# Four transformer layers on one core: half of the last output projection accumulated in PSUM ahead of the last group, and one wait for all norms

## The chip, the core and the metric

The kernel runs on one core of a Trainium2 chip. The core has a matrix engine (TensorE; in the profile PE for matmuls and PEld for weight loads), VectorE (DVE), ScalarE (ACT), GpSimd (POOL) and SyncE (SP), which issues transfers. They share SBUF; TensorE writes its results to PSUM, eight banks of 128 x 512 floats, which VectorE and ScalarE read. Each engine runs its own instructions in order and waits on semaphores for the others.

The metric is the device time of one execution in microseconds (us), the median of several runs: 2148.82 us before.

## What is computed

One sequence of 2048 rows with 640 features goes through four layers, A, B, A, B, each with a layer norm, an attention of 32 heads of 20 features, an output projection and a residual. Layer kind A lets a row see the last 256 rows only, kind B all rows. Shortened:

```python
def _B_ref(x, wqkv, wo):          # _A_ref: the same, with a window of 256
    qkv = (x @ wqkv).reshape(B, S, 3, H, Dh)
    q, k, v = ...
    scores = jnp.einsum("bhqd,bhkd->bhqk", q, k) * (Dh ** -0.5)
    p = _softmax(scores, axis=-1)
    o = jnp.einsum("bhqk,bhkd->bhqd", p, v)
    return o.transpose(0, 2, 1, 3).reshape(B, S, D) @ wo

x = x + _A_ref(_layernorm(x, axis=-1), A_wqkv, A_wo)
x = x + _B_ref(_layernorm(x, axis=-1), B_wqkv, B_wo)
x = x + _A_ref(_layernorm(x, axis=-1), A_wqkv, A_wo)
x = x + _B_ref(_layernorm(x, axis=-1), B_wqkv, B_wo)
```

## The kernel before

**Tiling.** Rows are cut into 4 chunks (c) of 512, a chunk into 4 row blocks (qb) of 128. Heads are cut into 8 groups (g) of 4 heads. In SBUF a group's 4 heads of 20 features stand on 4 strips of 32 partitions; small matmuls with 32 columns of weights go to the four strips of a bank side by side (the helper `by_columns`, L317 to L321). A unit of attention is one (layer, chunk, group), or a part of its keys; layers 1 and 3 see all keys, 64 score blocks of 128 keys x 512 queries for a whole unit.

**The main loop** (L1442) goes through the units in a fixed order, written out at L780 to L796, and one pass is a tile: 2 to 4 score blocks. A tile's scores go to PSUM banks 0 to 2 (even tiles) or 3 to 5 (odd tiles; a fourth block in bank 6), ScalarE turns them into exponentials with one instruction (L1515), and two or three tiles later the product with the values is summed in bank 7 (`op`, L1547). At a unit's end `finish_unit` copies bank 7 to SBUF (L924) and pushes a tail. Besides, VectorE computes some of the exponentials itself, by a chain of cheap instructions, two blocks at a time (the "side" blocks: L1031 reads the scores, L1047 to L1069 do the rest). A block is given to it only when a count of VectorE's backlog kept while the program is written (`state["lag"]`) is low and, from layer 3, chunk 1 on, when bank 6 is free.

**Tasks.** All else is a Python generator that yields after a few instructions: tails first, then `todo` in the order of need. `pump` (L271) advances them in each tile as far as a credit allows: `yield ("pe", n)` and `("hold", n)` cost n, after a hold the same task goes on at once, and `("wait", n)` puts the task to sleep for n tiles. So the program is one fixed order of instructions for each engine; a wait of a task is no semaphore, it only sets how far down in the order the next instructions stand. From layer 3, chunk 1 on the credit is 0.45 a tile. A task that needs a PSUM bank takes it from `mfree` with `take_m` (L286): from the end of the early stage that is bank 6 alone, and after the last tiles banks 1 to 5 as well (L1612). `keep_clock` and `warm_bank` put matmuls in whose result is not read, so that TensorE stays busy.

**The norm** (`t_ln`, L434): GpSimd computes 1/sqrt(variance + eps) in two instructions (L441, L444), the task sleeps 4 tiles in layers 0 and 1 and 2 tiles in layers 2 and 3 (L445), then VectorE computes the shift (L447) and the normed rows (L455), TensorE transposes them (L475) and VectorE copies them out. Then follow the value pieces (`t_v`) and the projections to keys and queries (`t_block`), whose results GpSimd writes to DRAM (L532, L575) and SyncE loads as units need them (L820 to L842).

**The tail of a unit** (`t_tail`, L1169): the sums of the softmax stand among the outputs; TensorE gathers them with selector strips (`sel4`), VectorE takes reciprocals (L1191) and splits each into two bf16 numbers (L1195, L1196), TensorE transposes them (L1204), VectorE copies (L1211), TensorE spreads them over the strips (`spread8`), and VectorE multiplies (L1232). In the very last tail `fill` puts dummy matmuls into bank 0 between these steps: 2, 3, 1 and 3. `settle` (L1237) then packs the strips of layer 3's later chunks densely with small transfers, and groups 6 and 7 of the last chunk stay in strips.

**The output projection** (`t_out`, L585) of a chunk sums over all groups for each row block and each half (i) of 320 output columns, adds the residual on VectorE (L607), and in layer 3 SyncE stores the row block (L613). For the last chunk it is cut in two: after group 5 is packed, `t_before_last` (L621) sums groups 0 to 5 in four dense matmuls for each of 8 pieces (L630), adds the residual and puts the float sums in `part_o` (L639); after the last group `t_out` does groups 6 and 7 with 8 strips a piece and adds them.

Of the kernel before, what the change touches and what calls it, by code (L numbers as in the profile page):

```python
# [15 lines left out]
ALU = mybir.AluOpType  # L16
ACT = mybir.ActivationFunctionType

P = 128
S = 2048  # L20
D = 640
# [3 lines left out]
KD = D // P  # L25
G = 8
C = 512
NC = S // C
EPS = 1e-5
SCALE = DH ** -0.5  # L30
HD = D // 2
# [27 lines left out]
def kernel(  # L59
# [10 lines left out]
    nc = tc.nc  # L70
# [22 lines left out]
    xout = out.flatten_outer_dims().rearrange("(t p) d -> p t d", p=P)  # L93
# [27 lines left out]
    op = ps[:, 7, :]  # L121
# [21 lines left out]
    def packed(l, c):  # L143

        return l == 3 and c > 0
# [58 lines left out]
    ready = set()  # L204
# [112 lines left out]
    def by_columns(out_, lhsT, rhs, start, stop):  # L317

        for j in range(lhsT.shape[-1] // 32):
            r = slice(32 * j, 32 * j + 32)  # L320
            nc.tensor.matmul(out_[r], lhsT=lhsT[:, r], rhs=rhs, start=start, stop=stop)  # L321
# [112 lines left out]
    def t_ln(l, c):  # L434
# [7 lines left out]
            out=rstd[:], in0=mv[:, :, 1], scalar1=EPS, scalar2=1.0, op0=ALU.add, op1=ALU.mult  # L442
        )
        nc.gpsimd.tensor_tensor(out=rstd[:], in0=rstd[:], in1=nhalf[:], op=ALU.pow)  # L444
        yield ("wait", 4 if l < 2 else 2)  # L445
        nmr = lnp.tile([P, 4], F32, name="nmr", tag="nmr")
        nc.vector.scalar_tensor_tensor(  # L447
            out=nmr[:], in0=mv[:, :, 0], scalar=-1.0, in1=rstd[:], op0=ALU.mult, op1=ALU.mult
# [136 lines left out]
    def t_out(l, c):  # L585
        on = ons[l, c]
        last = (l, c) == (3, NC - 1)
        while last and "before_last" not in ready:
            yield ("wait", 1)
        assert out_seq[out_n[0]] == l % 2  # L590
        dense = packed(l, c) and not last
        a, b = (0, KD) if dense else (G - 2 if last else 0, G)
        for qb in range(4):
            for i in range(2):
                mb = yield from take_m()
                yp = ps[:, mb, 0:HD]
                for g in range(a, b):
                    by_columns(
                        yp, on[:, g, qb * P : (qb + 1) * P],
                        wop[:, g, i * HD : (i + 1) * HD], g == a, g == b - 1,  # L600
                    )
                    if g < b - 1:
                        yield ("hold", 0.14)
                xv = x_sb[:, 4 * c + qb, i * HD : (i + 1) * HD]
                had = part_o["t"][:, 2 * qb + i, 0:HD] if last else xv
                state["lag"] += 0.5
                nc.vector.tensor_tensor(out=xv, in0=had, in1=yp, op=ALU.add)  # L607
                drop_m(mb)
                yield ("pe", 0.14)
            if l < 3:  # L610
                stats(l + 1, c, qb)
            else:
                nc.sync.dma_start(out=xout[:, 4 * c + qb, :], in_=x_sb[:, 4 * c + qb, :])  # L613
        ons.pop((l, c))
        ready.add(("out", l, c))
        ready.add(("x", l + 1, c))
        n = out_n[0] = out_n[0] + 1
        if n < len(out_seq) and (n == 13 or out_seq[n] != out_seq[n - 1]):
            load_wop(out_seq[n], n >= 13)

    def t_before_last():  # L621

        on = ons[3, NC - 1]
        for qb in range(4):
            for i in range(2):
                mb = yield from take_m()
                yp = ps[:, mb, 0:HD]
                for b in range(4):
                    n = min(P, (G - 2) * 80 - b * P)
                    nc.tensor.matmul(  # L630
                        yp, lhsT=on[0:n, b, qb * P : (qb + 1) * P],
                        rhs=wop[0:n, b, i * HD : (i + 1) * HD],
                        start=(b == 0), stop=(b == 3),
                    )
                    if b < 3:
                        yield ("hold", 0.14)
                xv = x_sb[:, 4 * (NC - 1) + qb, i * HD : (i + 1) * HD]
                state["lag"] += 0.5
                nc.vector.tensor_tensor(  # L639
                    out=part_o["t"][:, 2 * qb + i, 0:HD], in0=xv, in1=yp, op=ALU.add  # L640
                )
                drop_m(mb)
                yield ("pe", 0.14)
        ready.add("before_last")

    def push_layer(l, c):

# [521 lines left out]
    def t_tail(us):  # L1169
        final = us[-1][0:3] == (3, NC - 1, G - 1)  # L1170

        def fill(count):

            for n in range(count * final):
                nc.tensor.matmul(  # L1175
                    ps[:, 0, :], lhsT=ident[:], rhs=masks[:, 0, :], start=True, stop=True
                )

        n = len(us)
        yield ("wait", 2)  # L1180
# [56 lines left out]
    def settle(l, c, g, oT):  # L1237
# [128 lines left out]
    with tc.manual_schedule():  # L1366
# [75 lines left out]
        while ended is None or t < ended + 8:  # L1442
# [204 lines left out]
```

## Time and profile before

| | |
|---|---|
| median of 3 runs | 2148.82 us (2148.77 to 2149.24) |
| profiled execution, its own time | 2151.47 us |
| its span, first to last instruction | 2149.8 us |
| mean granted TensorE clock | 0.998 |
| ScalarE, exponentials (L1515) | 2052.5 us in 1643 instructions |
| side blocks of VectorE (L1031) from 522 us on | 307 |
| last exponential ends | 2138.55 us |
| last add of the projection ends | 2146.80 us |

The page of the profile has the busy time of each engine, the span in 40 slices, the DMA queues, the chain of work that ended last and the costliest groups of instructions. A group's line reads: source line, engine, operation, output and inputs by name, shape, count, then busy us and mean ns of one, then idle time of the engine just before and what ended it. Other answers from the same trace are used too: waits by engine, the timeline of an engine in a stretch (start us, duration us, instruction, and in brackets idle time before it), and busy times by stretch, where after the stretch and its length come PE, PEld, DVE, ACT and POOL with the number of instructions, the granted clock, the busy share of DMA and GB/s.

### The profile page before, as it was taken

The numbers are of one execution on the slowest core, as the hardware profiler recorded it, in microseconds if no ns is written. First come the engines' busy times: TensorE is split into PE (matmuls) and PEld (weight loads), VectorE is DVE, ScalarE is ACT, GpSimd is POOL, SyncE is SP. The second block draws the span as 40 slices with busy tenths as digits, with TensorE's granted clock in tenths as the row PEclk, the third lists the DMA queues.
The fourth block names the chain that finished last, engine by engine and source line by source line (L and its number), as shares of the span: only waits on it lengthen the run. The fifth ranks groups of instructions, "written<-read, shape, count | busy, mean of one in ns | idle before, by whom it ended". The sixth has DMA issues, their size and how long they took to land. (4 is left out here: it accounts for less than half of the span.)

```text
span 2149.8 us, 73242 instructions
## 1 busy us (share of the span) xinstructions
PE 1925.2 (90%) x31735; PEld 755.9 (35%) x31736; DVE 1445.1 (67%) x2699; ACT 2088.4 (97%) x1723; POOL 366.2 (17%) x808
## 2 busy tenths in 40 slices
PE   8999999988899888888988989898898988888898
PEld 4444443433333333333333433343322222222222
DVE  5566664426677676776767643773588888887886
ACT  7899999999999999999999999999999999999998
POOL 6553433100130003300033001510000000000000
PEclk9999999999999999999999999999999999999999
DMA  6422221321210112111220112111121111111100
GB/s 203 124 76 54 75 60 51 77 66 43 62 47 25 54 53 78 29 33 47 57 82 21 38 55 76 33 48 52 54 63 39 33 36 42 33 33 42 44 25 16
DMA packets 84080, 117.07 MB, mean 54 GB/s; under 512 B 21646, under 2 KB 65966, under 8 KB 83758
## 3 DMA queue, kind: packets, MB, share of 16 engines
q1 hardware_dynamic: 73598, 82.05, 14.5%
q0 software_dynamic: 10160, 30.36, 4.0%
q8 instruction: 248, 4.06, 0.8%
q14 instruction: 74, 0.61, 0.1%
HBM read 77.56 MB, written 28.77 MB: 49 GB/s over the span
## 5 line engine op out<-in xcount | busy, mean ns | idle before, releaser
L1515 ACT ACTIVATE pt<-ps 128x1536 bf16<-128x1536 f32 (+3 forms) x1643 | 2052.5, 1413 | 33.6 <-PE ps L1489 24.5
L1489 PE MATMUL ps<-qt,kt 32*128 32x512 bf16 x3913 | 545.7, 384 | 62.3 <-ACT pt L1515 54.9
L321 PE MATMUL ps<-masks,ident 128*32 128x512 bf16 x5720 | 512.3, 384 | 92.8 <-ACT pt L1515 47.8
L1547 PE MATMUL ps<-pt,vt 128*21 128x512 bf16 x3782 | 377.7, 386 | 0.3 <-ACT pt L1515 0.2
L1489 PEld LDWEIGHTS <-kt 32*128 32x128 bf16 x3913 | 155.4, 91 | 460.2 <-issue 441.6
L321 PEld LDWEIGHTS <-ident 128*32 128x32 bf16 x5720 | 182.2, 94 | 282.6 <-issue 256.5
L1587 POOL TENSOR_SCALAR_AFFINE_SELECT pt<-pt 128x256 bf16<-128x256 bf16 (+2 forms) x513 | 221.3, 453 | 199.6 <-ACT pt L1515 183.5
L1547 PEld LDWEIGHTS <-vt 128*21 128x21 bf16 x3782 | 93.7, 89 | 256.4 <-issue 253.0
L354 DVE CAST st<-ps 128x512 bf16<-128x512 f32 x128 | 88.4, 691 | 138.1 <-PE ps L321 138.0
L321 PE MATMUL ps<-wop,on 128*32 128x320 bf16 x3712 | 161.6, 300 | 4.4 <-DVE on L1232 2.2
L1031 DVE TENSOR_SCALAR spare<-ps 128x512 int32<-128x512 f32 x200 | 137.4, 687 | 29.9 <-PE ps L1013 27.1
L321 PEld LDWEIGHTS <-on 128*32 128x32 bf16 x5760 | 122.6, 95 | 62.3 <-issue 28.9
L1598 DVE TENSOR_TENSOR pt<-pt,masks 128x512 bf16<-128x512 bf16 (+3 forms) x275 | 117.7, 445 | 32.2 <-ACT pt L1515 30.9
L1489 PE MATMUL ps<-qa,ka 32*128 32x384 bf16 (+2 forms) x1408 | 119.7, 276 | 19.7 <-ACT pt L1515 16.4
L321 PE MATMUL ps<-xnT,spare 128*32 128x512 bf16 x1870 | 128.6, 381 | 3.5 <-ACT xnT L351 0.8
L1232 DVE TENSOR_TENSOR on<-on,ps 128x512 bf16<-128x512 bf16 x128 | 86.6, 685 | 65.1 <-PE ps L321 61.9
L321 PE MATMUL ps<-wv,xnT 128*32 128x320 bf16 x2560 | 115.9, 301 | 9.5 <-DVE on L1232 3.5
L607 DVE TENSOR_TENSOR x_sb<-x_sb,ps 128x320 bf16<-128x320 bf16 x120 | 58.4, 486 | 98.2 <-PE ps L321 97.0
L1031 DVE TENSOR_SCALAR raw_o<-ps 128x512 int32<-128x512 f32 x114 | 78.3, 687 | 52.5 <-PE ps L1489 51.7
L924 DVE CAST on<-ps 128x512 bf16<-128x512 f32 x112 | 76.9, 687 | 47.0 <-PE ps L1547 41.0
L321 PE MATMUL ps<-xnT,wqk 128*32 128x512 bf16 x1360 | 92.3, 381 | 1.7 <-DVE st L354 0.5
L575 POOL DMA_DIRECT2D k_d<-st x79 | 43.9, 556 | 258.8 <-DVE st L354 234.8
(110 smaller groups left out, 1711.6 us busy)
## 6 DMA issues: line engine op xcount, KB each, us to landing
vt<-v_d SPq DMA_DIRECT2D x48, 336.0 KB
kt<-k_d SPq DMA_DIRECT2D x192, 80.0 KB
k_d<-st POOLq DMA_DIRECT2D x78, 128.0 KB, 2.2
q_d<-st POOLq DMA_DIRECT2D x78, 128.0 KB, 2.1
qt<-q_d SPq DMA_DIRECT2D x384, 20.0 KB
v_d<-vs POOLq DMA_DIRECT2D x16, 336.0 KB, 3.1
qa<-q_d SPq DMA_DIRECT2D x248, 20.0 KB
ka<-k_d SPq DMA_DIRECT2D x248, 20.0 KB
```

The costliest lines, as they stand in the source:

```text
L321: nc.tensor.matmul(out_[r], lhsT=lhsT[:, r], rhs=rhs, start=start, stop=stop)
L354: nc.vector.tensor_copy(out=out_, in_=in_)
L575: nc.gpsimd.dma_start(out=dst, in_=staging.pop()[0 : rows.stop - rows.start])
L607: nc.vector.tensor_tensor(out=xv, in0=had, in1=yp, op=ALU.add)
L924: nc.vector.tensor_copy(out=oT, in_=op)
L1031: nc.vector.tensor_scalar(out=xi.bitcast(I32)[:, i * C : (i + 1) * C], in0=z, scalar1=SCALE * LOG2E * FIX, scalar2=127.5 * FIX, op0=ALU.mu ...
L1232: nc.vector.tensor_tensor(out=oT, in0=oT, in1=zb, op=ALU.mult)
L1489: nc.tensor.matmul(sp[:, i, col * P : (col + qn) * P], lhsT=u.k(kc, j), rhs=u.q(j, q0, qn), start=True, stop=True,)
L1515: nc.scalar.activation(out=pt[:, i:k, b0 * P :], in_=sp[:, i:k, b0 * P :], func=ACT.Exp, scale=SCALE,)
L1547: nc.tensor.matmul(op[32 * j : 32 * j + VW, q0 * P : (q0 + qn) * P], lhsT=u.v(kc, j), rhs=pg[:, i, col * P : (col + qn) * P], start=(first ...
L1587: nc.gpsimd.affine_select(out=v, in_=v, compare_op=ALU.is_gt if later else ALU.is_ge, fill=0.0, base=0, pattern=[[0, k - i], [-1 if later ...
L1598: nc.vector.tensor_tensor(out=pt_[:, i:k, cols], in0=pt_[:, i:k, cols], in1=mv_, op=ALU.mult)
```

## The change

1. **Norms.** The sleep in `t_ln` is 4 tiles in all layers; it was 2 in layers 2 and 3.
2. **Early sums.** `t_before_last` is pushed after group 6 is settled, not after group 5. It does the lower halves only (4 pieces, columns 0 to 319), each with the four dense matmuls of groups 0 to 5 and then four strips of group 6.
3. **Upper halves.** A new generator, `upper_halves`, fills banks 1 to 4, one for each row block: the residual by a matmul with the identity, the four dense matmuls, and the strips of group 6: 24 steps. `fill` in the last tail now takes three of these steps where it put one dummy (6, 9, 3 and the rest).
4. **The end.** A new `t_last` takes the place of `t_out` for the last chunk. For each row block it adds the four strips of group 7 to the upper half in its bank and ScalarE copies that to the output row; four strips of group 7 give the lower half, which VectorE adds to the early sum. Then the row block is stored.
5. After the last tiles `mfree` gets banks 0 and 5, not 1 to 5.

```diff
-        yield ("wait", 4 if l < 2 else 2)
+        yield ("wait", 4)
...
     def t_out(l, c):
         on = ons[l, c]
         last = (l, c) == (3, NC - 1)
-        while last and "before_last" not in ready:
-            yield ("wait", 1)
+        if last:
+            while "before_last" not in ready:
+                yield ("wait", 1)
+            yield from t_last(on)
+            return
...
+    def early_groups(yp, qb, i, start):
+        on = ons[3, NC - 1]
+        q, f = slice(qb * P, (qb + 1) * P), slice(i * HD, (i + 1) * HD)
+        def dense(b):
+            n = min(P, (G - 2) * 80 - b * P)
+            nc.tensor.matmul(
+                yp, lhsT=on[0:n, b, q], rhs=wop[0:n, b, f], start=start and b == 0, stop=False,
+            )
+        def strips():
+            by_columns(yp, on[:, G - 2, q], wop[:, G - 2, f], False, start)
+        return [lambda b=b: dense(b) for b in range(4)] + [strips]
+
     def t_before_last():
-        on = ons[3, NC - 1]
+        while ("tail", 3, NC - 1, G - 3) not in ready:
+            yield ("wait", 1)
         for qb in range(4):
-            for i in range(2):
...
+            mb = yield from take_m()
+            yp = ps[:, mb, 0:HD]
+            for n, step in enumerate(early_groups(yp, qb, 0, True)):
+                step()
+                if n < 4:
+                    yield ("hold", 0.14)
+            state["lag"] += 0.5
+            nc.vector.tensor_tensor(
+                out=part_o["t"][:, qb, 0:HD], in0=x_sb[:, 4 * (NC - 1) + qb, 0:HD], in1=yp,
+                op=ALU.add,
+            )
+            drop_m(mb)
+            yield ("pe", 0.14)
         ready.add("before_last")
+
+    def upper_halves():
+        for qb in range(4):
+            yp = ps[:, 1 + qb, 0:HD]
+            nc.tensor.matmul(
+                yp, lhsT=ident[:], rhs=x_sb[:, 4 * (NC - 1) + qb, HD:D], start=True, stop=False,
+            )
+            yield
+            for step in early_groups(yp, qb, 1, False):
+                step()
+                yield
+    upper = upper_halves()
+
+    def t_last(on):
+        for _ in upper:
+            pass
+        for qb in range(4):
+            row = 4 * (NC - 1) + qb
+            lhsT = on[:, G - 1, qb * P : (qb + 1) * P]
+            yp = ps[:, 1 + qb, 0:HD]
+            by_columns(yp, lhsT, wop[:, G - 1, HD:D], False, True)
+            nc.scalar.copy(out=x_sb[:, row, HD:D], in_=yp)
+            mb = yield from take_m()
+            yp = ps[:, mb, 0:HD]
+            by_columns(yp, lhsT, wop[:, G - 1, 0:HD], True, True)
+            nc.vector.tensor_tensor(
+                out=x_sb[:, row, 0:HD], in0=part_o["t"][:, qb, 0:HD], in1=yp, op=ALU.add
+            )
+            drop_m(mb)
+            nc.sync.dma_start(out=xout[:, row, :], in_=x_sb[:, row, :])
+            yield ("pe", 0.27)
+        ready.add(("out", 3, NC - 1))
...
         def fill(count):
-            for n in range(count * final):
-                nc.tensor.matmul(
-                    ps[:, 0, :], lhsT=ident[:], rhs=masks[:, 0, :], start=True, stop=True
-                )
+            for n in range(3 * count * final):
+                next(upper, None)
...
-        if (l, c, g) == (3, NC - 1, G - 3):
-            push("before_last", t_before_last(), 0, 8.0)
+        if (l, c, g) == (3, NC - 1, G - 2):
+            push("before_last", t_before_last(), 0, 5.0)
...
-        mfree.update((b, (0, 0)) for b in range(1, 6))
+        mfree.update((b, (0, 0)) for b in (0, 5))
```

More of the change, by code (lines that the diff above doesn't have):

```diff
@@ L587, in t_out @@
         last = (l, c) == (3, NC - 1)
-        while last and "before_last" not in ready:
-            yield ("wait", 1)
+        if last:
[3 more added lines that the diff above has]
+            return
         assert out_seq[out_n[0]] == l % 2
-        dense = packed(l, c) and not last
-        a, b = (0, KD) if dense else (G - 2 if last else 0, G)
+        a, b = (0, KD) if packed(l, c) else (0, G)
         for qb in range(4):
@@ L604, in t_out @@
                 xv = x_sb[:, 4 * c + qb, i * HD : (i + 1) * HD]
-                had = part_o["t"][:, 2 * qb + i, 0:HD] if last else xv
                 state["lag"] += 0.5
-                nc.vector.tensor_tensor(out=xv, in0=had, in1=yp, op=ALU.add)
+                nc.vector.tensor_tensor(out=xv, in0=xv, in1=yp, op=ALU.add)
                 drop_m(mb)
```

18 lines of the change are left out of this document (removed).

## The prediction, made before the changed kernel ran

> **What bounds the kernel now.** I began with the page's busy times. ScalarE, which turns score tiles into exponentials (L1515), is the engine nearest to full; its share is over the whole span, so I then asked for its idle time stage by stage and only at the end for the chain of waits of the last 12 us. A line of the first view reads: engine, busy us, share, instructions.
>
> ```profile
> PE 1925.2 (90%) x31735; PEld 755.9 (35%) x31736; DVE 1445.1 (67%) x2699; ACT 2088.4 (97%) x1723; POOL 366.2 (17%) x808
> ```
>
> While scores flow, then, a change is worth only what it adds to or takes from ScalarE's idle time, or the blocks that VectorE takes from it. One block of 512 columns costs ScalarE (1529 - 1081) = 0.45 us, from the mean 1536- and 1024-column exponentials. From 522 us (the first norm that the diff touches) to 1545 us ScalarE is busy 1009.54 of 1023 us, from 1545 to 2119 us 571.10 of 574. So the late norms can win back at most 13.5 us in their own stage, and the projection at the very end works where ScalarE has nothing left to do.
>
> **The late norms.** The view of waits by engine shows three waits of VectorE at L447 for GpSimd's power; listed by time these are 3 of the 8 norms of layers 2 and 3 (two-tile wait), at 698.9, 1209.3 and 1423.2 us. None of the 7 norms of layers 0 and 1 that run in this task (four-tile wait) has one. Around the second, the timelines of VectorE, TensorE and ScalarE, each with the idle time before an instruction and what ended it in brackets:
>
> ```profile
> DVE nmr L447 <- POOL rstd L444: 3.8, 3, 1.4
> ...
> 1209.26 0.16 DVE L447 SCALAR_TENSOR_TENSOR nmr<-mv,rstd 128x4 f32<-128x4 f32 x1 [1.44 <-POOL rstd L444]
> ...
> 1210.08 0.46 PE L475 MATMUL ps<-ident,xn 128*32 128x128 bf16 x20 [0.91 <-DVE xn L455]
> ...
> 1213.22 1.02 ACT L1515 ACTIVATE pt<-ps 128x1024 bf16<-128x1024 f32 x1 [0.80 <-PE ps L1489]
> 1215.70 1.45 ACT L1515 ACTIVATE pt<-ps 128x1536 bf16<-128x1536 f32 x1 [1.45 <-PE ps L1489]
> 1218.17 5.17 ACT L1515 ACTIVATE pt<-ps 128x1536 bf16<-128x1536 f32 x4 [1.02 <-PE ps L1489]
> ```
>
> The reader is to see a relay: GpSimd late, VectorE idle 1.44 us, TensorE idle 0.91 us for the normed row, and two us later ScalarE idle three times, 0.80 + 1.45 + 1.02 = 3.27 us, for scores. Why so much later and so much more? Busy time by stretch, with the granted clock behind the engines:
>
> ```profile
> 1207.00:1211.00 4.00, 2.68 (x49) 1.05 (x46) 2.49 (x8) 4.00 (x5) 1.85 (x4) 1.00 0.70 149
> 1211.00:1217.50 6.50, 6.26 (x95) 2.92 (x90) 2.77 (x6) 3.90 (x4) 0.00 (x0) 0.51 0.09 18
> ```
>
> TensorE was busy only 2.68 of 4.00 us, and then ran 6.5 us at clock 0.51, busy 6.26 of them, while ScalarE was busy 3.90. The halved clock turned a 0.91 us hole into 3.27 us.
>
> The page "TensorE: Matmul & The Clock Gate" of the Trainium skill (Part 1: The HAM clock gate) ties the half clock to at least one idle window of about 3.4 us. Here no idle of that length precedes it: the longest is 0.91 us, so the measurement decides. By the page's rule this hole would not be the cause, and the norms' term below would be 0; that case is the second rival.
>
> *What the four-tile wait does.* No instruction is added. L447, four normed rows (L455), 80 transposes (L475) and four copies are issued two tiles later, 2 x 1.3 = 2.6 us by the pitch of the exponentials (13 in 16.72 us from 690.58). GpSimd's pair (0.19 + 1.04 us) stays where it is and has 2.6 us more. Behind the norm move the value pieces, ten projected blocks, GpSimd's 10 k_d and q_d transfers (and 2 of v_d in layer 3), and SP's loads that read them. Cover: after the norm at 1209 the first k_d transfer leaves at 1232.87 and SP loads the next full unit from 1233.00; the unit before it is closed by VectorE at 1257.44. Twenty us of cover against 2.6. Without it each late us is a us of ScalarE's. Cost taken: 0. Gain taken: the 3.27 us; the other two waits (698.9 and 1423.2) cost ScalarE nothing within 5 us. Bounds: 0 (the hole comes back elsewhere) and 3.27 plus the idle that is left in the two stretches 1205 to 1247 (4.3 in all) and 1421 to 1451 (1.8 + 0.7), which is -6.8.
>
> **The end.** From the chain of waits and the timeline after the last exponential:
>
> ```profile
> 2139.50 0.69 DVE L924 CAST on<-ps 128x512 bf16<-128x512 f32 x1 [1.75 <-PE ps L1547]
> 2140.45 0.82 PE L1175 MATMUL ps<-masks,ident 128*128 128x512 bf16 x3
> 2141.33 0.23 PE L1204 MATMUL ps<-ident,hl 128*32 128x128 bf16 x1
> 2142.95 2.36 PE L321 MATMUL ps<-wop,on 128*32 128x320 bf16 x64
> 2143.53 3.27 DVE L607 TENSOR_TENSOR x_sb<-raw_o,ps 128x320 bf16<-128x320 f32 x8 [0.52 <-PE ps L321]
> 2144.44 2.72 SPq L613 DMA_DIRECT2D out_dram<-x_sb  x4
> ```
>
> TensorE finishes the projection in 2.36 us; eight adds of VectorE take 3.27 and set the end at 2146.80, and the last transfer the rest to 2149.8. ScalarE is idle.
>
> *Removed:* four of the eight adds. Their pitch is (3.27 - 0.48) / 7 = 0.40, so four end 4 x 0.40 = 1.60 us sooner: **-1.60**. *Added on ScalarE:* four copies of 128x320 float to bf16; the early copies of that form (L351, va<-ps) take 0.43 us, so 4 x 0.43 = 1.72 beside four adds of 3 x 0.40 + 0.48 = 1.68, starting four matmuls earlier: hidden, 0; without that lead they cost some 0.05. *Removed on TensorE:* 32 of the 64 strips, not on the path, 0.
>
> *Added on TensorE, ahead of it:* the nine dummies (pitch (0.82 - 0.39) / 2 = 0.215) become 24 real steps. A step is a 320-column matmul, pitch 0.135 from L630 ((0.72 - 0.45) / 2), or four strips at (2.36 - 0.30) / 63 x 4 = 0.13. The path through the final tail then shifts so:
> - Two dummies (0.43) become 6 steps (0.81): +0.38, of which 0.10 was idle before the selector strips at 2140.25: shift 0.28.
> - Three (0.645) become 9 (1.215): +0.57; TensorE was free at 2140.45 + 0.645 = 2141.10 and the transpose began at 2141.33, so 0.23 is absorbed: shift 0.62.
> - One becomes 3: +0.19, of which 0.16 was idle before the spread strips at 2141.86: 0.65.
> - Three become the 6 that are left: +0.165, of which 0.10 idle before 2142.95: 0.72.
>
> So the projection starts at 2143.67, the first add 0.58 later as now, and the last ends at 2143.67 + 0.58 + 1.20 + 0.48 = 2145.93 instead of 2146.80: **-0.87**. Banks 0, 5 and 6 rotate over four lower halves; the fourth waits for the first add, ended by 2144.73, when TensorE needs the bank at about 2144.7: 0. Bounds: -1.60 (no shift) and +0.7 (the full shift, and copies that hold the last transfer as eight adds did).
>
> *Moved:* the early sums start after group 6 instead of group 5, so at about 2128.4 (two tiles after L1232 at 2126.89) instead of 2120.67, four sums of 0.68 us of TensorE instead of eight of 0.56. At rate 0.45 a tile against a cost of 0.70 that is four sums in five tiles, done near 2134, with the last scores at 2137.26; ScalarE is busy 19.50 of 19.50 us here, which hides both versions. Without those three us the rest of a sum (0.7) would land in the tail. VectorE's four adds fewer (4 x 0.49) and a free bank 6 allow between no and two more blocks off ScalarE (0 to -0.90): I take one, **-0.45**. No transfer is added; SP's four output stores stay behind the second half of each row.
>
> **Sum.** -3.27 - 0.87 - 0.45 = -4.6 us. The profiled execution took 2151.47 us, 1.67 of it outside its span of 2149.8; less 4.6 that is 2146.9. The median of the runs, 2148.82, lies 2.65 below the profiled execution, so **2144.2 us**. What this sum can't price is the order: from 522 us on every tile's choice of task, and with it the 307 blocks that VectorE takes, may fall otherwise; six blocks are 2.7 us. Own range 2141.0 to 2147.5.
>
> **Rivals.**
> 1. *More starvation goes with the wait.* The waits at L447 also put VectorE's chain of exponentials late, and the idle left over in 1205 to 1247 and 1421 to 1451 (6.8 - 3.27 = 3.5 us) goes too: 2144.2 - 3.5 = 2140.7. For: at 1432.72 TensorE waits 0.33 us for L1069 of that chain. Against: ten us lie between.
> 2. *The norms are worth nothing*: the clock halves anyway in the new order, as it also does shortly after 1351 us with no norm near, or the hole has another cause. The end alone: 2148.8 - 0.87 - 0.45 = 2147.5. The skill's rule named above leads here.
> 3. *Slower: TensorE waits for normed rows.* L447 and L455 now stand behind two more tiles of VectorE's block chain (L1069 0.68, L1031 0.68), while the transposes still follow only one tile, 1.3 us, later. Where VectorE is more than that behind, TensorE idles, as it did 0.78 us at 82.52 us after a four-tile norm, and the clock halves. Each such place costs 3.27. It decides from the third of the eight norms on: two more than now, 6.5, less 1.3 from the end, 2154.0. Against: the other six four-tile norms show no such wait of half a us or more.
>
> **Chances.** Forecast 0.48, rival 1 0.22, rival 2 0.12, rival 3 0.18. A measurement of this kernel can tell about 0.2%, 4.3 us, from no change: below 2144.5 is faster. That holds rival 1 and 0.27 of the forecast: 0.49. Within: the rest of the forecast, 0.21, and rival 2: 0.33. Slower 0.18. The range goes from rival 1's side with some blocks more, 2139.0, to 2152.5, which leaves out the larger part of rival 3.
>
> **What would show it.** Right: no wait of VectorE at L447; clock 1.00 through the stretch after the norm near 1208 us and no ScalarE idle over 0.5 us there; four adds and four copies at the end, the first add some 3.7 us after the selector strips begin (3.3 now), the last one's end about 6.4 us after L924's final cast begins (7.3 now); four early sums finished before the last score. Wrong: rows at clock 0.5 with ScalarE idle beside them at other norms; fewer blocks at L1031; an early sum or a copy that ends after the last add.

## The result, and the profile after

The changed kernel takes **2154.15 us** (median of 16 runs, 2153.38 to 2155.18), the kernel before 2149.53 in the same comparison (16 runs, 2148.45 to 2151.95): a ratio of 1.0019, 95% interval 1.0012 to 1.0026. It is slower by 4.1 us by the ratio (4.6 us between the medians), where 4.6 us less than before were forecast. The profiled execution of the changed kernel has a span of 2152.4 us (before 2149.8).

Executions of one and the same kernel differ in how long TensorE runs at half clock. In one of the two largest comparisons, 19 executions of the kernel before with a mean granted clock of 0.999 or more have a median of 2148.58 us, the 14 with 0.998 or less one of 2150.97; the profiled execution of before (0.998, 2151.47 us) belongs to the second group. The mean does not say where in the span the half clock fell: in the 20 traces of this case it stands near 80, 793, 899, 1211, 1350 and 1488 us, for 3.41 or 6.83 us each time.

**The whole span.** The line of busy times of the changed kernel, and the same line of the changed kernel with the two-tile wait of before put back (experiment e3_end_only below, span 2146.0 us, no half clock near 1209 us). The two programs differ in nothing but the wait.

```profile
PE 1929.3 (90%) x31847; PEld 758.3 (35%) x31847; DVE 1447.7 (67%) x2697; ACT 2091.4 (97%) x1726; POOL 366.2 (17%) x807
```
```profile
PE 1921.1 (90%) x31755; PEld 754.2 (35%) x31755; DVE 1446.6 (67%) x2698; ACT 2089.4 (97%) x1726; POOL 365.6 (17%) x808
```

ScalarE runs 1726 instructions in both. Idle is span less busy: 61.0 us after, 56.6 with the wait back, 4.4 more; and the same instructions are busy 2.0 us longer. From the view of waits by engine (us in total, times, longest us), ScalarE waiting for scores, after and then with the wait put back:

```profile
ACT pt L1560 <- PE ps L1534: 25.7, 72, 1.3
```
```profile
ACT pt L1560 <- PE ps L1534: 21.4, 59, 1.3
```

Thirteen more waits, none longer: many small starvations, not one new stall. (In the kernel before the same wait reads 61 times, 24.5 us; 3.27 of these are the half-clock stretch that the prediction shows.)

**After the norm near 1209 us**, the stretch that the prediction built on. Busy time by stretch, after:

```profile
1207.00:1211.00 4.00, 3.63 (x64) 1.56 (x61) 2.89 (x6) 3.71 (x4) 0.00 (x0) 1.00 0.24 58
1211.00:1217.50 6.50, 5.29 (x97) 2.23 (x93) 6.00 (x14) 6.50 (x6) 2.33 (x4) 1.00 0.45 93
```

Clock 1.00, ScalarE busy 10.21 of 10.50 us. No wait of VectorE at L447 is left in the view of waits. What was to be removed has been removed.

**Where a late norm now crowds.** The norm of layer 2's third chunk, around 1040 us. VectorE's timeline of before and then of after (start us, duration us, instruction, idle time before it in brackets), the first copy of transposed rows and the value pieces that follow:

```profile
1039.45 0.15 DVE L447 SCALAR_TENSOR_TENSOR nmr<-mv,rstd 128x4 f32<-128x4 f32 x1
...
1049.76 0.49 DVE L354 CAST va<-ps 128x320 bf16<-128x320 f32 x1 [1.02 <-PE ps L321]
...
1054.13 0.48 DVE L354 CAST va<-ps 128x320 bf16<-128x320 f32 x1
...
1067.08 0.48 DVE L354 CAST va<-ps 128x320 bf16<-128x320 f32 x1
```
```profile
1046.62 0.15 DVE L447 SCALAR_TENSOR_TENSOR nmr<-mv,rstd 128x4 f32<-128x4 f32 x1
...
1051.69 0.48 DVE L354 COPY xnT<-ps 128x640 bf16<-128x640 bf16 x1
1052.94 0.36 DVE L1236 RECIPROCAL rz<-ps 128x32 f32<-128x32 f32 x1 [0.77 <-PE ps L321]
...
1060.37 0.49 DVE L354 COPY xnT<-ps 128x640 bf16<-128x640 bf16 x1 [0.78 <-PE ps L475]
...
1066.33 0.49 DVE L354 CAST va<-ps 128x320 bf16<-128x320 f32 x1 [0.96 <-PE ps L321]
1067.79 0.49 DVE L354 CAST va<-ps 128x320 bf16<-128x320 f32 x1 [0.96 <-PE ps L321]
...
1073.75 0.49 DVE L354 CAST va<-ps 128x320 bf16<-128x320 f32 x1 [0.96 <-PE ps L321]
```

Before, the eight value pieces lie spread over 17.3 us (1049.76 to 1067.08), with a unit's tail between them. After, a tail falls among the four copies of the norm instead (1052.94 is its reciprocal), the copies take 8.7 us from first to last (4.3 before), and the eight pieces follow in 11.9 us (1061.82 to 1073.75).

The forecast moved the norm by 2.6 us. Counted against equal numbers of score columns read (after and the end alone), GpSimd's power itself comes 2.5 us later here, the shift (L447) 4.8, the fourth copy 9.9 and the first value piece 9.6. At the other seven norms of layers 2 and 3 the first value piece comes 0.2 to 3.1 us later. ScalarE's timeline in the same two stretches:

```profile
1037.77 22.83 ACT L1515 ACTIVATE pt<-ps 128x1536 bf16<-128x1536 f32 x18
1060.76 15.77 ACT L1515 ACTIVATE pt<-ps 128x1536 bf16<-128x1536 f32 x12 [0.17 <-PE ps L1489]
```
```profile
1053.27 11.41 ACT L1560 ACTIVATE pt<-ps 128x1536 bf16<-128x1536 f32 x9 [0.16 <-PE ps L1534]
1065.12 6.76 ACT L1560 ACTIVATE pt<-ps 128x1536 bf16<-128x1536 f32 x5 [0.43 <-PE ps L1534]
1072.54 6.65 ACT L1560 ACTIVATE pt<-ps 128x1536 bf16<-128x1536 f32 x5 [0.66 <-PE ps L1534]
1079.36 2.79 ACT L1560 ACTIVATE pt<-ps 128x1536 bf16<-128x1536 f32 x2 [0.17 <-PE ps L1534]
```

Before, 30 exponentials run nearly without a gap; after, 19 from 1053.27 on have gaps of 0.43, 0.66 and 0.17 us before the next. Counted in score blocks, before reads one in about 0.46 us (some 84 in 38.8), after one in 0.49 (53 in 26.1): where each tile has a value piece the pieces follow at 1.46 us (1066.33, 1067.79), while full exponentials start 1.33 us apart in the median. The stretch between 1020 and 1110 us is the dearest of all. From the two traces I took the times by which equal numbers of score columns had been read by ScalarE or VectorE. From 500 us on, after falls behind the kernel with the two-tile wait by, in us:

| up to (us) | 840 | 940 | 1020 | 1110 | 1190 | 1260 | 1400 | 1545 | 2090 |
|---|---|---|---|---|---|---|---|---|---|
| lost in the stage | 1.74 | 0.0 | -0.3 | 2.75 | -1.2 | 1.5 | 0.6 | -0.2 | 0.6 |
| in all | 1.7 | 1.7 | 1.4 | 4.2 | 3.0 | 4.5 | 5.1 | 4.9 | 5.5 |

Another 0.75 us lie before 500 us, where the two programs are the same, and are the luck of these two executions; the last exponential ends at 2141.42 and 2135.19, 6.23 apart.

Counted the same way, the kernel before falls 2.6 us behind the end alone between 1190 and 1260 us, and in no other stage from 500 to 2090 us by more than 0.04. So its half clock near 1211 us cost 2.6 us, not the 3.27 us of idle time that the prediction took for the price.

**The end**, on the timelines of TensorE, VectorE, ScalarE and SP after:

```profile
2141.80 0.31 PE L662 MATMUL ps<-x_sb,ident 128*128 128x320 bf16 x1
2141.91 0.69 DVE L971 CAST on<-ps 128x512 bf16<-128x512 f32 x1 [0.76 <-PE ps L1592]
2142.95 0.25 PE L321 MATMUL ps<-sel,on 128*32 128x4 bf16 x16
2144.68 0.23 PE L1249 MATMUL ps<-ident,hl 128*32 128x128 bf16 x1
...
2146.48 1.57 PE L321 MATMUL ps<-wop,on 128*32 128x320 bf16 x36
2146.99 1.41 ACT L681 CAST x_sb<-ps 128x320 bf16<-128x320 f32 x4 [5.56 <-PE ps L321]
2147.19 1.68 DVE L685 TENSOR_TENSOR x_sb<-raw_o,ps 128x320 bf16<-128x320 f32 x4 [0.69 <-PE ps L321]
2147.74 1.91 SPq L689 DMA_DIRECT2D out_dram<-x_sb  x4
```

The first add stands 4.24 us behind the selector strips (3.28 before), the last ends 6.96 us behind the start of the final cast (7.30 before). From the last exponential to the end of the span it is 10.93 us; before it is 10.73 (ScalarE's timeline of before ends at 2139.04; the 2138.55 of the table above is where the chain of waits leaves ScalarE).

So the span's +2.6 us is made of +5.5 (the wait), -2.6 (the half clock near 1211 us that this execution did not have), -0.55 (two side blocks more), +0.2 (the end) and +0.1 (before 500 us, where after and before are nearly level). In the medians the second is nearly absent.

### The profile page after: what moved, and what is told of

The parts are those of the page before. It is cut to its first block, busy times and chain, and to the rows that moved or that the text cites. A ratio compares the mean times of both kernels' runs of the same rounds, so it can differ in the third digit from the quotient of the medians.

```text
span 2152.4 us, 73456 instructions
## 1 busy us (share of the span) xinstructions
PE 1929.3 (90%) x31847; PEld 758.3 (35%) x31847; DVE 1447.7 (67%) x2697; ACT 2091.4 (97%) x1726; POOL 366.2 (17%) x807
## 4 chain that ended last, share of the span: by engine, by line
ACT 49%; PE 30%; issue 14%; DVE 7%; POOL 1%; ACTq 0%; DVEq 0%; POOLq 0%
ACT pt L1560 48%; PE ps L321 16%; PE ps L1534 8%; PE ps L1592 4%; DVE on L1277 1%; DVE raw_o L1078 1%; DVE st L354 1%; PE ps L1060 1%; DVE pt L1643 0%; POOL pt L1632 0%; PE ps L475 0%; DVE xnT L354 0%; DVE x_sb L608 0%; DVE on L971 0%; PE ps L1359 0%
## 5 line engine op out<-in xcount | busy, mean ns | idle before, releaser
L321 PE MATMUL ps<-masks,ident 128*32 128x512 bf16 x5836 | 520.8, 383 | 88.5 <-ACT pt L1560 49.3
L1632 POOL TENSOR_SCALAR_AFFINE_SELECT pt<-pt 128x128 bf16<-128x128 bf16 (+2 forms) x512 | 221.1, 454 | 204.5 <-ACT pt L1560 188.3
L1643 DVE TENSOR_TENSOR pt<-pt,masks 128x768 bf16<-128x768 bf16 (+3 forms) x274 | 119.3, 451 | 28.2 <-ACT pt L1560 27.0
```

The lines of the kernel that those rows point to most:

```text
L1632: nc.gpsimd.affine_select(out=v, in_=v, compare_op=ALU.is_gt if later else ALU.is_ge, fill=0.0, base=0, pattern=[[0, k - i], [-1 if later ...
L1643: nc.vector.tensor_tensor(out=pt_[:, i:k, cols], in0=pt_[:, i:k, cols], in1=mv_, op=ALU.mult)
```

## The experiments

Theory A, after the result: the four-tile wait alone costs the 5 us, by crowding, and the end is worth nothing. Theory B: the rebuilt end costs it. Theory C: the wait is harmless, and it is the order of all later work that the two together shift. All times are medians in us; "before" is the kernel before in the same comparison.

**The kernel before once more, and each half of the change alone.** The first has no edit. The second is the kernel before with

```diff
-        yield ("wait", 4 if l < 2 else 2)
+        yield ("wait", 4)
```

and the third the changed kernel with this line as it was.

> The kernel before, unchanged, run many times, to see whether the half clock after the norm at 1209 us is in every execution. Theory 'sometimes': it depends on how the execution falls against the clock's own window, so the times fall into two groups, some 2148.5 to 2149.5 us and some 2151 to 2152 us, the upper group with a mean granted clock lower by about 0.001 to 0.002 (6.8 us at half speed in 2150 is 0.0016). Theory 'always' (the prediction's): one group, all with the same mean clock, and the two levels have another cause.

> The kernel before with the four-tile wait alone; the end as before. Theory 'norms': the later norms crowd their projections and starve ScalarE, nearly all of the loss is here: 2153.5 to 2155.0 us, and no level 2.6 us apart. Theory 'end': the loss comes from the new end: 2148.0 to 2149.5 us.

> The changed kernel with the wait of layers 2 and 3 put back to two tiles. Theory 'norms': the order up to 2110 us is that of before, so its two levels come back, 2148 to 2149.5 and about 2151; the end is worth -0.5 to +0.3 us. Theory 'end': 2153 us or more.

| | median (range, runs) | ratio to before (95%) |
|---|---|---|
| before again | 2148.53 (2147.94 to 2151.70, 11) | 0.9998 (0.9989 to 1.0007) |
| wait alone | 2153.73 (2153.33 to 2154.87, 11) | 1.0020 (1.0011 to 1.0029) |
| end alone | 2149.43 (2147.95 to 2152.14, 11) | 1.0000 (0.9991 to 1.0009) |

The wait carries the whole loss; the end is worth nothing that can be told. And the two others show what the half clock was. In the profile of the end alone, with the wait and the hole of before in place, the stretches before and after the norm's rows read:

```profile
1206.00:1210.00 4.00, 2.68 (x49) 0.94 (x41) 2.49 (x8) 4.00 (x4) 1.85 (x4) 1.00 0.69 158
1210.00:1216.50 6.50, 5.99 (x133) 2.87 (x134) 4.83 (x11) 6.04 (x6) 0.00 (x0) 1.00 0.11 21
```

and TensorE's and ScalarE's timelines in them:

```profile
1209.40 0.46 PE L475 MATMUL ps<-ident,xn 128*32 128x128 bf16 x20 [0.91 <-DVE xn L455]
...
1213.22 6.85 ACT L1560 ACTIVATE pt<-ps 128x1536 bf16<-128x1536 f32 x5 [0.34 <-PE ps L1534]
```

The same 2.68 us of 4.00, the same hole of 0.91 us, clock 1.00 behind it, and 0.34 us of ScalarE's instead of 3.27. In the repeated kernel before:

```profile
1211.00:1217.50 6.50, 5.58 (x101) 2.57 (x105) 4.33 (x10) 4.53 (x5) 0.45 (x2) 0.74 0.27 53
```

a part of the stretch, 3.41 us from 1213.19 on, is at half clock. This execution (2151.70 us) has two more such parts, near 80 and 899 us, and the one near 899 cost it 1.0 us by the count above: a slower execution need not owe its time to this hole. Seven of the kept traces have the hole (0.91 or 0.92 us); the clock halves behind it in two of them and not in the other five. What decides is in the last section.

**One layer alone, and other lengths.** In the line above, for layer 2 alone `4 if l < 3 else 2`, for layer 3 alone `4 if l != 2 else 2`, and 1, 3 or 6 tiles in place of the 2 of layers 2 and 3.

> The kernel before with four tiles for layer 2's norms only; layer 3 keeps two. Theory 'norms of layer 2': most of the loss is here, 2151.5 to 2154.5 us, with ScalarE idle in the stretches after 1050 and 815 us as in the changed kernel. Theory 'interplay' (neither layer's wait costs alone, only the order that both make): 2147.5 to 2150 us, as layer 3's wait alone did.

> The kernel before with four tiles for layer 3's norms only; the three waits of VectorE at the norm were all in layer 3. Theory 'norms of layer 2' (the traces' loss after the norms of layer 2 is 0.4 to 2 us each, after those of layer 3 less): 2147.5 to 2150.0 us, one level, no half clock near 1210 us. Theory 'any order but the old one is worse by chance': 2151 us or more, with ScalarE idle after layer 3's norms.

> The kernel before with a one-tile wait for the norms of layers 2 and 3. Theory 'later costs' (each tile of wait moves the projections nearer to their due time and crowds them): no slower than before in ScalarE's idle time, but VectorE waits at the norm's shift in more than three of eight norms: 2146 to 2150 us. Theory 'order by chance': anywhere between 2146 and 2155 us.

> A three-tile wait for the norms of layers 2 and 3. Theory 'later costs': between two and four tiles, 2149.5 to 2152.5 us. Theory 'order by chance': not between them, or not in line with 1 and 6.

> A six-tile wait for the norms of layers 2 and 3. Theory 'later costs': more than with four tiles, 2156 us or more. Theory 'order by chance': the loss of four tiles (5 us) need not be there, 2147 to 2155 us.

| wait in layers 2 and 3 | median (runs) | ratio (95%) | waits at L447 |
|---|---|---|---|
| 1 tile | 2156.31 (6) | 1.0030 (1.0018 to 1.0042) | 4 |
| 2 (before, in the comparison of 1, 3 and 6) | 2149.53 (25) | | 3 |
| 3 | 2150.59 (10) | 1.0002 (0.9993 to 1.0011) | 1 |
| 4 | 2153.73 (11) | 1.0020 (1.0011 to 1.0029) | 0 |
| 6 | 2155.55 (8) | 1.0028 (1.0017 to 1.0038) | 0 |
| 4 in layer 2 alone | 2151.70 (10) | 1.0007 (0.9997 to 1.0016) | 2 |
| 4 in layer 3 alone | 2148.63 (11) | 0.9999 (0.9990 to 1.0007) | 0 |

Waits of VectorE for the power go with each tile more, as they should. From two tiles on the median rises with each length, though the step from 2 to 3 lies within its interval; there it is lateness that costs, not waiting. Six tiles fell between the two forecasts. One tile is dear as well and lies above the ranges of both theories: its profile has a hole of 1.40 us and 6.8 us at half clock near 1212 us, where it loses 5.2 us to the end alone; 2.3 us more, lost between 1400 and 1545 us, are not explained.

In the traces, from 500 to 2090 us and against the end alone, layer 2's norms lose 2.6 us (2.9 of it between 1020 and 1110 us, with gains elsewhere), layer 3's 0.4, and the two together 5.4, more than their sum: what the order does behind one norm depends on the others. A single stage moves with the order too: layer 3 alone is 1.7 us ahead by 1020 us and has given it back by 1110. One level of times was expected of layer 3 alone, which has no hole near 1210 us; yet 3 of its 11 runs lie at 2150.6 to 2151.8 us, so that hole is not the only source of slower executions.

**Where the late pieces land.** Theory A in two sharper forms. A1: the late value pieces fall into tiles of two score blocks, in which TensorE has no room. A2: they collide with a unit's tail for bank 6, as in the stretch shown. For A1 no task starts in a two-block tile of the later layers, with the wait of two and of four tiles:

```diff
             r = rate(t)
+            if n_b == 2 and woven < state["unit"] < final and not narrow(units[state["unit"]]):
+                saved, state["credit"] = state["credit"], -1.0
+                pump(0.0, 0.0)
+                keep_clock()
+                state["credit"] = min(saved + r, r + 0.1)
+                return
```

For A2 the norm's rows in layers 2 and 3 go ahead of the tails (`state["norm"]` is set from the first normed row to the last copy), again with four tiles and with two:

```diff
-            if t.wake <= state["tick"]:
+            if t.wake <= state["tick"] and not state["norm"]:
```

> The kernel before (two-tile wait) with one rule more: in layers 1 to 3 up to the last stage no background piece is started in a tile whose exponential has only two blocks. Pieces beside two-block tiles cost ScalarE 0.3 us each over its pitch in the traces so far (some 32 of them, 9 us); beside three-block tiles 0.08. Theory 'pieces beside short tiles': 2143 to 2147 us. Theory 'lateness': the pieces left out are crowded elsewhere, 2148 to 2154 us.

> The same rule with the four-tile wait. Theory 'pieces beside short tiles': the distance from the two-tile wait falls from 5.2 us to under 2.5. Theory 'lateness itself': it stays at 4 us or more.

> The four-tile wait, and while a norm of layer 2 or 3 has its four rows in hand no step of a unit's tail goes ahead of it. With four tiles the norm near 1050 us fell among the steps of a tail (both need bank 6), its four copies took 8.7 us instead of 4.3, and the eight value pieces behind it ran one a tile. Theory 'collision with the tail': the loss between 1020 and 1110 us (2.75 us against two tiles) falls under 1.0 and the median to 2150.5 to 2152 us. Theory 'crowding by the due time alone': that loss stays at 2 us or more, 2152.5 us or more.

> The same rule with the two-tile wait, as a control. There the norm met the tail in one tile only: within 1 us of before, 2147.5 to 2150.5 us, under either theory.

| | median (runs) | ratio (95%) |
|---|---|---|
| no start in two-block tiles, wait 2 | 2148.75 (11) | 0.9996 (0.9987 to 1.0005) |
| the same, wait 4 | 2152.56 (11) | 1.0016 (1.0007 to 1.0024) |
| norm ahead of tails, wait 2 | 2149.32 (10) | 1.0000 (0.9991 to 1.0010) |
| the same, wait 4 | 2154.33 (10) | 1.0025 (1.0016 to 1.0034) |

A1 does not carry it: with the pieces kept out of two-block tiles the wait still costs 3.8 us (2152.56 less 2148.75), between the two forecasts and near the second. In the trace of the two-tile version, set beside the end alone from 500 to 1545 us, the time by which exponentials start later than at the usual pitch fell behind tiles of two blocks (13.5 to 8.7 us) and rose behind tiles of three (16.0 to 19.1). Nor does the loss belong to the stretch shown above: under this rule the wait of four loses 0.7 us to that of two between 1020 and 1110 us, and 2.9 between 840 and 1020. A2, as far as it is about the copies of the norm, falls. With four tiles and the norm first, VectorE's timeline has the copies back at their old pace, and yet the tail only moves on, in among the value pieces:

```profile
1051.90 0.48 DVE L354 COPY xnT<-ps 128x640 bf16<-128x640 bf16 x1
...
1055.71 0.49 DVE L354 COPY xnT<-ps 128x640 bf16<-128x640 bf16 x1 [0.78 <-PE ps L476]
...
1064.09 0.49 DVE L354 CAST va<-ps 128x320 bf16<-128x320 f32 x1 [0.72 <-PE ps L321]
1065.12 0.68 DVE L1234 TENSOR_TENSOR on<-on,ps 128x512 bf16<-128x512 bf16 x1
...
1074.04 0.49 DVE L354 CAST va<-ps 128x320 bf16<-128x320 f32 x1 [0.96 <-PE ps L321]
```

3.8 us for the four copies instead of 8.7, the last piece at 1074.04 (1073.75 in the changed kernel), and 2.83 us lost between 1020 and 1110 us instead of 2.75. That the tail costs as much among the value pieces is not excluded.

**The due time.** Common to all of these is that the work behind the norm starts later while the unit that needs it stays where it is. The task rate is worked out from a margin of 16 tiles ahead of that unit; with 12, the same work gets four tiles more. Wait four and wait two:

```diff
-                    r = max(r, done / max(starts[id(units[task.need])] - now - 16, 1))
+                    r = max(r, done / max(starts[id(units[task.need])] - now - 12, 1))
```

> The four-tile wait, and the pace of the background work is worked out for 12 tiles before the due unit instead of 16. Theory 'crowding by the due time': the four tiles given back let the pieces stand apart again; the loss falls to 2.5 us or less, 2148.5 to 2151 us. Theory 'collision': a looser due time does not move the norm from the tail by itself; 2152 us or more.

> The same pace with the two-tile wait. Theory 'crowding by the due time': as fast as before or faster, 2145 to 2149 us. Theory 'order by chance' (any other order than that of before costs some us): 2150.5 us or more.

With four tiles 2152.14 (10 runs; ratio 1.0012, 1.0002 to 1.0021), with two 2150.86 (10 runs; 1.0005, 0.9996 to 1.0015). The wait now costs 1.3 us instead of 4 to 5, although the median kept to the forecast of 'collision' (2152 or more). Between 1020 and 1110 us 0.84 us are lost to the end alone instead of 2.75, and the control loses 1.4 there: beside its control the late version is 0.6 us ahead in this stretch, with its first value piece 6.1 us later. What it loses to the control, 4.8 us, lies between 680 and 840 us, where this one execution has 6.8 us at half clock from 792.86 on; over all other stages from 500 to 2090 us it is 2.3 ahead. That is what crowding asks for: the same lateness costs nothing where the work has more room. But the control is itself 1.5 us dearer than before (2149.40 in this comparison; the interval holds no change), loses 2.7 us between 500 and 680 us, and came out as 'order by chance' had forecast. So another reading stands beside it: the order of before is a good one among its neighbours, and each change that moves all later tasks tends to a worse one. The runs do not part the two.

**The end.** Two forms that ask what bounds it. In the end alone the last store goes out on ScalarE's queue:

```diff
-            nc.sync.dma_start(out=xout[:, row, :], in_=x_sb[:, row, :])
+            (nc.scalar if qb == 3 else nc.sync).dma_start(out=xout[:, row, :], in_=x_sb[:, row, :])
```

> The changed end with the two-tile wait, and the last row block's store issued by ScalarE's queue instead of SP's. SP issues the four stores 0.49 us apart and the last starts 0.38 us after the last add. Theory 'SP is the last link': from the last exponential to the end 0.3 to 0.5 us less than 10.8. Theory 'not': 10.7 or more.

2149.26 (10 runs; ratio 0.9999, 0.9990 to 1.0008). The last store is issued 7.52 us behind the last exponential instead of 7.77, but the span ends at 10.84 (10.78): from this queue it takes 3.32 us to the end instead of 3.0, and 0.69 us to issue instead of 0.39. Taking the last store off SP's queue gains nothing.

The other form shortens TensorE's path. The kernel before keeps its eight early sums of groups 0 to 5; in the last tail each upper half is loaded by one matmul with the identity and four strips of group 6, 8 steps for 24, and the upper early sums are rounded to bf16 for it:

```diff
+        for qb in range(4):
+            yp = ps[:, 1 + qb, 0:HD]
+            nc.tensor.matmul(yp, lhsT=ident[:], rhs=early_sum(qb, 1), start=True, stop=False)
+            yield 1
+            by_columns(yp, on[:, G - 2, qb * P : (qb + 1) * P], wop[:, G - 2, HD:D], False, False)
+            yield 1
```

> The kernel before with another end: eight early sums as before, but those of the upper halves kept as bf16; in the last tail they enter PSUM by one identity matmul each and four strips of group 6 (8 steps instead of 24), group 7 follows, ScalarE copies the upper halves and VectorE adds the lower ones. Theory 'the 24 steps are in the way': the first add comes again some 4.0 us after the final copy of the outputs begins (before 4.03, changed kernel 5.28), from the last exponential to the end 10.0 us or less (before 10.7, changed kernel 10.8 to 10.9). Theory 'the stores bound the end alone': 10.6 us or more.

> The shortened end once more (before's order of norms, eight early sums, eight steps in the last tail), with more runs. If the 1.0 us between its undisturbed executions and those of before is its own: a median some 0.7 to 1.5 below before's of this call, ratio near 0.9995 with an interval that reaches below 1. If it was the luck of one call: within 0.4 of before's median.

> The shortened end with the four-tile wait in layer 3 alone. If the waits of the two layers only crowd where layer 2's value pieces meet their due time: as e16 within 0.5 us, with no wait of VectorE for a norm's power in layer 3. If any four-tile wait costs by its own two tiles: 2 us over e16 or more.

| | median (range, runs) | before | ratio (95%) |
|---|---|---|---|
| shortened end | 2148.26 (2146.98 to 2149.99, 10) | 2148.90 | 0.9996 (0.9987 to 1.0005) |
| once more | 2148.63 (2147.85 to 2151.33, 11) | 2149.91 | 0.9995 (0.9987 to 1.0004) |
| with 4 tiles in layer 3 | 2149.41 (2149.09 to 2150.43, 11) | 2149.91 | 0.9997 (0.9988 to 1.0006) |

In the first one's profile (VectorE, TensorE, SP):

```profile
2136.24 0.69 DVE L964 CAST on<-ps 128x512 bf16<-128x512 f32 x1 [1.75 <-PE ps L1589]
...
2139.78 1.81 PE L321 MATMUL ps<-wop,on 128*32 128x320 bf16 x48 [0.30 <-DVE on L1274]
2140.50 1.68 DVE L678 TENSOR_TENSOR x_sb<-raw_o,ps 128x320 bf16<-128x320 f32 x4 [0.77 <-PE ps L321]
2141.05 1.84 SPq L682 DMA_DIRECT2D out_dram<-x_sb  x4
```

The first add comes 4.26 us behind the final cast (5.28 after, 4.03 before), TensorE even waits 0.30 us for the last product, and from the last exponential to the end it is 9.75 us instead of 10.73. Both medians are below that of before, by 0.6 and 1.3 us; neither interval excludes no change. With layer 3's wait on top it is 0.8 dearer, outside the 0.5 us that were forecast and far from the 2 us of the other theory; no wait at L447 is left, and its range is the narrowest of the three (1.3 us). In its profile 0.7 us stand at the end: SP's second store takes 1.09 us to issue, 0.36 in the run without that wait. The shortened end by itself is the fastest form here, but not shown faster than before.

## Why the prediction was wrong

**The norms' gain, -3.27.** The chain was read rightly (L447 late, the hole, half clock, starvation), and the waits went. The step that failed is the sum: "The profiled execution took 2151.47 us ... less 4.6 that is 2146.9. The median of the runs, 2148.82, lies 2.65 below the profiled execution, so 2144.2 us." The half clock was what put that execution above the median. Its removal was counted once as a gain and once more in the shift. The price was also read too high: against the end alone, with the same hole at full clock, the half clock cost 2.6 us, which is the whole of those 2.65. And it is a price of single executions: of seven traces with the hole, five had nothing there to win. The rule of "TensorE: Matmul & The Clock Gate" in the Trainium skill (Part 1) that the activity window runs freely and its place changes from run to run bears on this, and the traces agree: the clock's changes lie on a grid of 3.41 us whose place is another in each execution, and the same hole of 0.91 us was followed by 6.83 us at half clock, by 3.41, or by none. Its other rule, at least one idle window before a half clock, still has the trace of before against it.

**The cover, "Cost taken: 0".** This made the sign wrong. Twenty us between the first k_d transfer and the unit that needs it were real, and no unit waited for its keys. But the cover was asked of the wrong followers. Behind the norm stand 80 transposes, eight value pieces and the projections, which need TensorE in the tiles themselves and, one after another, bank 6. They start later and are due as before. Nor did "two tiles later, 2 x 1.3 = 2.6 us" hold where it mattered: at the norm near 1040 us the first value piece came 9.6 us later. What was put at 0 measured +5.2 us in the medians (2153.73 less 2148.53; 4.0 less the larger set's 2149.70) and 5.4 in the trace of the wait alone, counted as in the table. That the wait alone carries the loss, that layer 2's norms carry the larger part of it in the traces, and that neither the collision with the norm's copies nor two-block tiles make it, the runs show. How much is crowding before the due time, for which the margin of 12 tiles speaks, and how much the luck of another order stays open.

**The bound, "at most 13.5 us".** ScalarE's idle time was taken for all that can be won or lost in that stage. It isn't: of the 6.4 us between the span after and that of the end alone, 2.0 are busy time. A full exponential lasts 1529 ns in the mean but starts 1.33 us after its predecessor (median of all), so it overlaps the next; one that starts late loses the overlap, and the loss is booked as work. The two traces bear this out: the exponentials' own durations add up to 2.5 us less after than in the end alone, and yet the time covered by them is 2.1 us more.

**The end, -0.87.** Measured +0.2 from the last exponential to the end, and in the runs of the end alone nothing. The four adds took 1.68 as forecast and the four copies were hidden. The shift of TensorE's path was mis-sized: 0.72 forecast, 1.25 measured (first add 5.28 behind the cast, 4.03 before). The 24 steps took 0.135 us each in the sum and 0.155 (six in 2141.80 to 2142.73) to 0.17 in the trace: 24 times 0.02 to 0.035 is the missing half us. And of the 0.34 that VectorE's last add then still gained, nothing reached the end: SP's last store is issued 0.39 us behind the last add's end (7.83 against 7.44 from the last exponential; 7.79 against 7.76 before). On another queue the end did not move either, so which step of a store sets it was not found.

**One block more, -0.45.** There were two (316 side blocks for 314), worth 0.55 us, inside the stated 0 to -0.90. The early sums came later than forecast: done some 5 us before the last exponential ends (near 2134, with the end at 2139.04), it said, and ahead of the last scores. Their last add starts at 2140.66, behind the last scores (2139.59 in TensorE's timeline) and 0.8 us before the last exponential ends. They stayed hidden, by less than was thought.

**The rivals.** The forecast of rival 3, 2154.0, is the number that came, by another way: TensorE waits for normed rows twice in the profile after (1.2 us in all), three times before (2.1), and the only half clock in the norms' stretch, near 1354 us, left ScalarE busy. Rival 2, norms worth nothing, was right about the gain; no rival had the cost of being late.

## What to carry to other kernels

Before a loss seen in one profile is put down as a gain, ask whether the runs have it: a profiled execution above the median may owe its distance to the very event, and then the two must not both be subtracted. A step that is moved back costs nothing only if everything behind it, and not just the last consumer, has room to move with it; work with a fixed due time that starts later stands denser, which is the likeliest price here, though the luck of the order was not excluded. Idle time of a pipelined engine is a lower bound of its starvation, since instructions that no longer overlap look busy.

## What the hardware showed

- **Half clock on a grid.** In the 15 traces with half clock inside the span, all changes of the clock there lie on a grid of 3.413 us to within 3 ns, and the grid stands elsewhere in each trace. Counted over all 20 traces by the profile's busy times: after each of the nine grid stretches at full clock in which TensorE was busy less than 0.60 of the time, the next one ran at half clock; between 0.60 and 0.71 it did after 12 of 154; above that after none of 12331.
- **What the grid makes of one hole.** With the same hole of 0.91 us, the grid stretch around it was busy for 1.99 of 3.42 us in the repeated kernel before (then 3.41 us at half clock), 2.09 of 3.41 in the profile of before (then 6.83 us, ScalarE idle 3.27), and 2.26 of 3.41 in the end alone (no half clock, ScalarE idle 0.34). The shortened end had 2.10 of 3.42 and no half clock, so the edge lies about there. Over 33 executions the two groups of times lie 2.4 us apart.
- **Overlap of exponentials.** 1288 exponentials of 128 x 1536 with a mean of 1529 ns were busy 1778.6 us in all, 0.148 us less each than their durations add to; where two overlap it is by 0.19 us in the mean. "ScalarE: Activation LUTs" in the Trainium skill (section "What ACT_TABLE_LOAD costs") has an overlap of about 93 ns for back-to-back activations; here the measurement is larger.
- **Queues.** The last store of 128 rows took 3.32 us from issue to the end of the span on ScalarE's queue, 3.0 on SP's.
